# Spreading the split of tile 3's tokens over nine slices, and reading tile 0's partial results back a slice earlier

## The chip, the cores and the metric

The kernel runs on one core of one Trainium2 chip. The metric is the device time of one execution, in microseconds (us). The engines are named as in the profile: PE (TensorE matmul), PEld (its weight loads), DVE (VectorE), ACT (ScalarE), POOL (GpSimd) and SP (SyncE, which here only issues DMAs). Each engine works through its own list of instructions in order and waits on semaphores for the others.

## The reference

A windowed attention (32 keys wide; in the upper half of the heads every fourth key) feeds a feed-forward layer with a PReLU. Everything is float32.

```python
# q, k, v: (8 batches, 8 heads, 576 positions, 64)
scores = where(mask, q @ k.T / 8, -1e9)            # mask by head: plain window or dilated window
attn_out = (softmax(scores) @ v)                   # rows of x: 4608 tokens x 512
h = x @ w_in                                       # 512 x 2048
g = maximum(h, 0) + alpha * minimum(h, 0)
out = g @ w_out                                    # 2048 x 512
```

## The kernel before

**Precision.** PE multiplies in a reduced float format. So every operand is split in two parts of that format: a high part (a copy with a cast, on ACT) and a low part (the value minus its high part, on DVE). A product is three matmuls: high by high, high by low, low by high (`PASSES`).

**Tiles.** The 4608 tokens are nine tiles of 512. Tiles 0 to 2 are computed directly, slice by slice. A *slice* is one block of 128 of the 2048 hidden features for one tile: 12 matmuls of 128x512 for h (L495, `ffn_h`), the PReLU on ACT and DVE (L503 and L508, or L515 and L516), the split of g (L521 high on ACT, L526 low on DVE), and 12 matmuls for y (L543, `ffn_y`). There are 48 slices, numbered n = 0 to 47 in the list `slices`: six of tile 0, sixteen of tile 1, the last ten of tile 0 (n = 22 to 31), then tile 2 (n = 32 to 47). Tiles 3 to 8 follow in pairs, in the *paired stage*. It computes the products of two tiles at once with seven block products in place of eight (`Seven`, `PRODUCTS`, L728 and L1029), and so needs sums and differences of the two tiles' tokens, each split in high and low.

**What runs beside the slices.** Attention runs ahead of the tiles that use it. A pair of heads is *scored* in one slice: its scores on PE (L266), masked maxima on DVE (L318, L321, twice each, for two halves), exponentials on ACT (L331). One slice later come the division and the transpose on DVE (L338 to L346, tile `pt`). The pair is *valued* in the next slice that scores, or the one set for it: the values on PE (L361, tile `o`), copied out by ACT (L415, L422) and stored to DRAM as `kept`. Near the end of the list the scored slices are 37, 38, 40, 41, 43, 44, the valued ones 38, 40, 41, 43, 44, 46. Beside that, POOL sums weights for the paired stage, and ACT and DVE split those sums (L601, L606, L626, L630).

**What sets the order.** The order of every engine's instructions is the order in which the program is written; the pools only add waits for buffers. In the loop `for n in range(CUT, NS)`, round n issues h of slice n+1, the PReLU and the split of slice n+1 and the division of the pair scored in round n-1, then y of slice n-1, then the scores and values of round n with their maxima, exponentials and copies, the work of the weights, and at its very end `late_ops[n]`. With `NS = 48`, `NS - 9` is round 39. The PE banks "a0" to "a3" go round among h, the two score banks and the two value banks. So with one h, two score and two value banks in a round, the h of the next round takes the bank of that round's first scores and must wait until L318 has read them.

**The split of tile 3's tokens.** `token_parts(3)` returns 18 steps in three lists (`zeroth`, `first`, `second`): with k0, k1 the halves of tile 3 and z0, z1 those of tile 4 (each 128x1024), it splits k0 (named B11), k1 (B21), T1 = z0 - k0, T3 = z1 - z0, T2 = z1 - k0, B22 = z1 and T4 = k1 - T2. A difference is one DVE instruction (L707), a high part one on ACT (L710), a low part one on DVE (L713). `plan_parts` puts these 18 steps at the ends of rounds. Tile 3's tokens are loaded from DRAM in round 36, tile 4's in round 41 (L1093, `reload`).

**Tile 0's partial results.** The first six slices of tile 0 leave their sum of y in DRAM (`part`). When the last slice of tile 0 is multiplied (its y is issued in round 32), four DMAs read it back into `ob` (L541), and the function `end`, run in the same round, adds it to y on DVE (L551) and writes the result out (L556). Tile 2's first y, in round 33, uses the same four banks and waits for these four additions.

Of the kernel before, what the change touches and what calls it, by code (L numbers as in the profile page):

```python
# [31 lines left out]
NC = DM // P  # L32
# [34 lines left out]
def tile_window_attention_prelu_ffn(  # L67
# [12 lines left out]
    nc = tc.nc  # L80
# [18 lines left out]
    part = dram.tile([NC, P, TT], F32, name="part")  # L99
# [8 lines left out]
    def bank(side, shape, name):  # L108
        n = turn[side]
        turn[side] = n + 1  # L110
        return psp.tile(shape, F32, tag=f"{side}{n % 4}", name=name)
# [23 lines left out]
    def weight(which, a, f):  # L135
        k = next(k for k, (first, end) in enumerate(SPANS) if first <= f < end)
        i = 2 * which + a
        if (i, k) not in places:
            places[i, k] = place(i, k)
        return places[i, k][:, f - SPANS[k][0], :]  # L140
# [342 lines left out]
    def results(t):  # L483
        if t not in result:
            result[t] = const.tile([P, NC, TT], F32, tag=f"{XTAGS[t]}0", name=f"ob_{t}")
        return result[t]
# [3 lines left out]
    def ffn_h(t, f, first=0, end=NC):  # L490
        if first == 0:
            ms[t, f] = bank("a", [P, TT], f"h_{t}_{f}")
        for c in range(first, end):
            for n, (a, e) in enumerate(PASSES):
                nc.tensor.matmul(  # L495
                    ms[t, f], lhsT=weight(0, a, f)[:, c * P:(c + 1) * P], rhs=half(t, c)[:, e, :],
                    start=(c == 0 and n == 0), stop=(c == NC - 1 and n == 2))
# [30 lines left out]
    def ffn_y(t, f):  # L528
        first = (t, f) in ((0, 0), (0, CUT), (1, 0), (2, HALF))
        if first:  # L530
            ys[t] = [bank("y", [P, TT], f"y_{t}_{f}_{c}") for c in range(NC)]
        g = gs.pop((t, f))
        cut, rest = (t, f) == (0, CUT - 1), t == 0 and f == NF - 1
        last = cut or (t, f) in ((0, NF - 1), (1, NF - 1), (2, HALF - 1))
        if last:
            o = [
                att.tile([P, TT], F32, tag=("k", "q", "v", "pt")[c], name=f"ob_{t}_{f}_{c}") if cut else
                results(t)[:, c] for c in range(NC)]
        for c in range(NC):
            if rest:  # L540
                nc.sync.dma_start(out=o[c], in_=part[c])  # L541
            for n, (a, e) in enumerate(PASSES):
                nc.tensor.matmul(  # L543
                    ys[t][c], lhsT=weight(1, a, f)[:, c * P:(c + 1) * P], rhs=g[:, e, :],
                    start=(first and n == 0), stop=(last and n == 2),
                )

        def end():
            for c in range(NC):
                if rest:  # L550
                    nc.vector.tensor_tensor(out=o[c], in0=ys[t][c], in1=o[c], op=ALU.add)  # L551
                elif c % 2:
                    nc.vector.tensor_copy(out=o[c], in_=ys[t][c])
                else:
                    nc.scalar.copy(out=o[c], in_=ys[t][c])
                nc.sync.dma_start(  # L556
                    out=part[c] if cut else outT[c * P:(c + 1) * P, t * TT:(t + 1) * TT], in_=o[c])

        if last:
            ended.append(end)  # L560
# [140 lines left out]
    def token_parts(t):  # L701


        k0, k1, z0, z1 = raw(t, 0), raw(t, 1), raw(t + 1, 0), raw(t + 1, 1)

        def diff(out, x, y):
            return lambda: nc.vector.tensor_tensor(out=out, in0=x, in1=y, op=ALU.subtract)  # L707

        def high(name, x):
            return lambda: nc.scalar.copy(out=part_of(name, 0), in_=x)  # L710

        def low(name, x):
            return lambda: nc.vector.tensor_tensor(  # L713
                out=part_of(name, 1), in0=x, in1=part_of(name, 0).bitcast(F32), op=ALU.subtract)

        zeroth = [high("B11", k0), low("B11", k0), high("B21", k1), low("B21", k1)]
        first = [diff(k0, z0, k0), high("T1", k0), low("T1", k0)]
        second = [
            diff(z0, z1, z0), high("T3", z0), diff(k0, z1, k0), high("T2", k0), low("T3", z0),
            diff(k1, k1, k0), low("T2", k0), high("B22", z1), high("T4", k1), low("B22", z1), low("T4", k1),  # L720
        ]
        return zeroth, first, second
# [434 lines left out]
    late_ops = {}  # L1157

    def plan_parts():
        zeroth, first, second = token_parts(NSTD)  # L1160
        late_ops[NS - 9] = zeroth[:2]
        late_ops[NS - 5] = zeroth[2:] + first
        late_ops[NS - 3], late_ops[NS - 2], late_ops[NS - 1] = second[:5], second[5:8], second[8:]


    slices = [(0, f) for f in range(CUT)] + [(1, f) for f in range(NF)] + [(0, f) for f in range(CUT, NF)]
# [1 line left out]
    NS = len(slices)  # L1168
# [183 lines left out]
    for n in range(CUT, NS):  # L1352
        scored, valued, divided = (at.get(n) for at in (score_at, value_at, divide_at))
        whole = n + 1 == 2 * NF
        for op in put.pop(n, ()):
            op()
        if SCRATCH <= n < SCRATCH + NF:
            save(n - SCRATCH)
        if n + 1 < NS and not whole:
            ffn_h(*slices[n + 1])  # L1360
        if n <= SECOND - 2:

            ffn_sum(*slices[n])
            ffn_high(*slices[n])
            for w in late:
                w.low()
            words = [op for w in now for op in w.words()]
            for op in words[:1]:
                op()
            ffn_low(*slices[n])  # L1370
            if divided and n < SECOND - 2:
                divided.divisions()
                divided.turns()
            for op in words[1:]:
                op()
            if n + 1 <= SECOND - 2:
                ffn_relu(*slices[n + 1])
            late, now = now, [conversion() for _ in range(quota.pop(0) if quota else 0)]
            ahead()
            for w in late:  # L1380
                w.high()
        elif late:
            late.pop().low()
        if whole:
            ffn_y(*slices[n - 1])
            ffn_h(*slices[n + 1])
        if SECOND - 2 <= n < NS - 1:
            if n - 1 in score_at:
                ffn_parts(*slices[n + 1])
            else:  # L1390
                ffn_relu(*slices[n + 1])
                ffn_sum(*slices[n + 1])
            ffn_high(*slices[n + 1])
            if divided:
                divided.divisions()
                divided.turns()
            ffn_low(*slices[n + 1])
        if not whole:
            ffn_y(*slices[n - 1])
        if n in split_at:  # L1400
            combined_high(split_at[n])
        if n in cast_at:
            others_high(cast_at[n])
        if scored:
            scored.scores()
            pairs[pairs.index(scored) + 1].load_qk()
        if valued:
            valued.values()
            pairs[pairs.index(valued) + 1].load_v()
        if n in split_at:  # L1410
            put[n + 1].append(lambda i=split_at[n]: combined_store(i))
        if scored:
            scored.maxima()
            scored.exponentials(0, 5)
        while ended:
            ended.pop()()
        if valued:
            valued.highs()
            put[n + 1].append(valued.keep)
        if scored:  # L1420
            scored.exponentials(5)
        if valued:
            valued.lows(nc.scalar.copy)
        if n in split_at:
            combined_low(split_at[n])
        if n in cast_at:
            others_low(cast_at[n])
            put[n + 1].append(lambda i=cast_at[n]: others_store(i))
        if n == HALF + 1:
            pairs[2 * NC].load_qk()  # L1430
            pairs[2 * NC].load_v()
        if n in combine_at:
            combine(combine_at[n], "xB1" if n < 2 * NF - 1 else "xA1")
        if n in other_at:
            others(other_at[n], "xB0" if n <= 2 * NF - 1 else "xA0")
        for t, at in ((NSTD, NS - 12), (NSTD + 1, NS - 7)):
            for c in range(NC if n == at else 0):
                reload(t, c)
        if n == NS - 9:
            half(NSTD + 1, 0)  # L1440
            plan_parts()
        if n == NS - 2:
            nc.sync.dma_start(out=mask_sb, in_=masks[:, NMASK:2 * NMASK])
        for op in late_ops.pop(n, ()):
            op()
        if n >= NS - NRING + 2:
            feed()
# [76 lines left out]
```

## Time and profile before

| | |
|---|---|
| median of three runs | 855.82 us (853.35, 855.82, 857.77) |
| the profiled execution | 853.31 us, of which the span from first to last instruction is 850.8 us |
| PE busy | 826.2 us (97% of the span) |
| DVE busy | 650.6 us (76%) |
| ACT busy | 466.6 us (55%) |
| DMA | 194.90 MB, mean 229 GB/s |
| mean granted TensorE clock | 0.945 |

PE is busy nearly all the time, so the time is PE's work plus PE's pauses. A row of the view in order of time reads: start in us, duration in us, engine, line, operation, names written and read, shape, how many in a row (x12), and in brackets how long the engine sat idle before it and what released it. The durations of matmuls are modelled and overlap the next ones, so starts are the safer numbers on PE. The paired stage starts at 367 us.

### The profile page before, as it was taken

To read this page: it belongs to the slowest core of one execution; us is meant where nothing else is said; L and a number is where in the kernel's file an instruction comes from. 1 tells how busy PE (TensorE), PEld (TensorE's weight loads), DVE (VectorE), ACT (ScalarE), POOL (GpSimd) and SP (SyncE) were. 2 spreads that over 40 slices of the span, in tenths; PEclk is the share of its full clock that TensorE was granted. 3 is DMA by queue.
4 is the path that set the end of the run, shared out by engine and by line. 5 is a ranking of instruction groups with operands and counts; after the bars stand their busy time and mean duration, and the time that the engine had idled before them with its cause. 6 is when DMAs were issued, how large, how long until landed. Compare 5 with 4: busy or idle time off the path is not lost.

```text
span 850.8 us, 20392 instructions
## 1 busy us (share of the span) xinstructions
PE 826.2 (97%) x8014; PEld 671.7 (79%) x8014; DVE 650.6 (76%) x1087; ACT 466.6 (55%) x1276; POOL 86.5 (10%) x88
## 2 busy tenths in 40 slices
PE   8889999999999999799999999999999999999998
PEld 5668888878877887687888788878887888888886
DVE  5997866867667787679966998897379988944983
ACT  6895766645534466367635752674176436624640
POOL 0000000214683552000000000000000000000000
PEclk9999999999999999899999999999999999999999
DMA  7862479679766769286799598856876886667664
GB/s 243 281 203 86 164 236 310 216 237 294 214 215 236 263 217 338 94 296 195 230 313 314 154 314 299 272 170 214 242 215 190 290 287 198 195 190 196 193 193 157
DMA packets 131485, 194.90 MB, mean 229 GB/s; under 512 B 11582, under 2 KB 67518, under 8 KB 131390
## 3 DMA queue, kind: packets, MB, share of 16 engines
q1 hardware_dynamic: 131390, 193.60, 71.6%
q8 instruction: 63, 1.03, 0.5%
q14 instruction: 32, 0.26, 0.1%
HBM read 145.33 MB, written 48.23 MB: 228 GB/s over the span
## 4 chain that ended last, share of the span: by engine, by line
PE 78%; DVE 11%; ACT 5%; issue 2%; DMA 2%; SPq 1%; DVEq 0%; ACTq 0%
PE h L495 15%; PE qA L1029 14%; PE y L543 13%; PE pA L728 11%; PE qC L1029 7%; PE pC L728 5%; PE qB L1029 4%; PE o L361 3%; PE pB L728 3%; ACT pr L331 2%; PE s L266 2%; DVE held L787 1%; DMA ws<-w_in 1%; DVE pr L340 1%; DVE stage L780 1%
## 5 line engine op out<-in xcount | busy, mean ns | idle before, releaser
L495 PE MATMUL h<-x,w_dt.float32r 128*128 128x512 f32 x576 | 143.9, 399 | 2.6 <-DVE pr L318 1.0
L543 PE MATMUL y<-g,w_dt.float32r 128*128 128x512 f32 x576 | 138.6, 390 | 1.1 <-DVE ob L551 1.1
L495 PEld LDWEIGHTS h<-x,w_dt.float32r 128*128 128x128 f32 x576 | 107.8, 190 | 26.5 <-DVE pr L318 1.4
L543 PEld LDWEIGHTS y<-g,w_dt.float32r 128*128 128x128 f32 x576 | 107.8, 188 | 24.4 <-DVE ob L551 1.1
L331 ACT ACTIVATE pr<-pr,nm 128x64 f32<-128x64 f32 x216 | 72.4, 338 | 25.8 <-DVE nm L321 25.8
L773 ACT COPY stage<-pA 128x512 f32<-128x512 f32 x72 | 42.3, 587 | 47.6 <-PE pA L728 46.9
L728 PE MATMUL pA<-parts_w,ring_w 128*128 128x512 f32 x234 | 58.2, 392 | 0.3 <-ACT stage L773 0.3
L837 ACT CAST gp<-held 128x512 fp32r<-128x512 f32 x60 | 37.2, 620 | 35.7 <-DVE held L833 35.5
L728 PE MATMUL pA<-parts_w,ring_xA 128*128 128x512 f32 x222 | 55.4, 393 | 0.7 <-ACT stage L773 0.7
L728 PEld LDWEIGHTS pA<-parts_w,ring_w 128*128 128x128 f32 x234 | 43.6, 188 | 9.9 <-ACT stage L773 0.7
L503 ACT ACTIVATE m<-h 128x512 f32<-128x512 f32 x33 | 19.7, 598 | 57.5 <-PE h L495 49.0
L521 ACT CAST g<-m 128x512 fp32r<-128x512 f32 x48 | 29.7, 618 | 39.2 <-DVE m L516 20.7
L728 PEld LDWEIGHTS pA<-parts_w,ring_xA 128*128 128x128 f32 x222 | 41.2, 188 | 10.5 <-ACT stage L773 2.0
L526 DVE TENSOR_TENSOR g<-m,g 128x512 fp32r<-128x512 f32 x48 | 37.3, 778 | 15.5 <-ACT g L521 15.5
L780 DVE TENSOR_TENSOR stage<-pC,stage 128x512 f32<-128x512 f32 x48 | 33.0, 688 | 13.4 <-ACT stage L773 8.3
L954 ACT COPY py<-qA 128x512 f32<-128x512 f32 x24 | 13.8, 588 | 52.0 <-PE qA L1029 51.2
L1029 PE MATMUL qA<-gp,ring_xA 128*128 128x512 f32 x174 | 42.3, 390 | 0.0
L842 DVE TENSOR_TENSOR gp<-held,gp 128x512 fp32r<-128x512 f32 x60 | 40.7, 687 | 1.6 <-ACT gp L837 1.6
L331 ACT ACTIVATION_READ_ACCUMULATOR pr<-pr,nm 128x1 f32 x216 | 40.9, 189 | 0.0
L958 DVE TENSOR_TENSOR py<-qC,py 128x512 f32<-128x512 f32 x24 | 16.0, 688 | 31.0 <-PE qC L1029 24.7
L1029 PE MATMUL qA<-gp,ring_w 128*128 128x512 f32 x162 | 39.5, 389 | 0.0
L1029 PEld LDWEIGHTS qA<-gp,ring_xA 128*128 128x128 f32 x174 | 32.6, 188 | 7.0 <-DVE gp L842 0.2
(188 smaller groups left out, 1703.8 us busy)
## 6 DMA issues: line engine op xcount, KB each, us to landing
ring_w<-wS SPq DMA_DIRECT2D x69, 256.0 KB, 3.0
ring_xA<-wS SPq DMA_DIRECT2D x66, 256.0 KB, 3.0
ring_xA<-wY SPq DMA_DIRECT2D x40, 256.0 KB, 3.6
ring_w<-wY SPq DMA_DIRECT2D x36, 256.0 KB, 3.6
ring_g<-wS SPq DMA_DIRECT2D x33, 256.0 KB, 3.2
wO<-w_dt.float32r SPq DMA_DIRECT2D x32, 256.0 KB, 4.1
wS<-wc SPq DMA_DIRECT2D x16, 512.0 KB, 4.5
ring_w<-wO SPq DMA_DIRECT2D x31, 256.0 KB, 3.2
```

What stands on the lines that cost most here:

```text
L331: nc.scalar.activation(out=self.pr[:, r, :], in_=self.ps[r // CUT0][:, r % CUT0, :] if self.onto else self.pr[:, r, :], func=AF.Exp, bias= ...
L361: nc.tensor.matmul(self.po[u][e * D:(e + 1) * D, a:z, :], lhsT=self.v[rows, i, :], rhs=self.pt[rows, a * BK + (BQ if i else 0):z * BK - (B ...
L495: nc.tensor.matmul(ms[t, f], lhsT=weight(0, a, f)[:, c * P:(c + 1) * P], rhs=half(t, c)[:, e, :], start=(c == 0 and n == 0), stop=(c == NC ...
L521: nc.scalar.copy(out=g[:, 0, :], in_=ms[t, f])
L526: nc.vector.tensor_tensor(out=g[:, 1, :], in0=ms.pop((t, f)), in1=g[:, 0, :].bitcast(F32), op=ALU.subtract)
L543: nc.tensor.matmul(ys[t][c], lhsT=weight(1, a, f)[:, c * P:(c + 1) * P], rhs=g[:, e, :], start=(first and n == 0), stop=(last and n == 2),)
L728: nc.tensor.matmul(to, lhsT=w[:, (2 * a + c) * P:(2 * a + c + 1) * P], rhs=part_of(name, e)[:, c * TT:(c + 1) * TT], start=start and c == ...
L773: nc.scalar.copy(out=self.s(n), in_=self.A)
L780: nc.vector.tensor_tensor(out=self.s(n), in0=getattr(self, src), in1=self.s(to), op=ALU.add)
L837: nc.scalar.copy(out=self.pair(n)[:, 0], in_=self.whole(n))
L842: nc.vector.tensor_tensor(out=p[:, 1], in0=self.whole(n), in1=p[:, 0].bitcast(F32), op=ALU.subtract)
L1029: nc.tensor.matmul(to(q)[c], lhsT=w[:, k * P:(k + 1) * P], rhs=rhs[:, e], start=(i, q) in firsts and n == 0, stop=i == GP - 1 and n == 2, ...
```

## The change

Two things move; no instruction is added or removed. First, the four reads of `part` are taken out of `ffn_y` (round 32) and issued at the start of round 31. Second, the steps of `token_parts(3)`, which stood in lots of 2, 5, 5, 3 and 3 in rounds 39, 43, 45, 46 and 47, are dealt to all rounds from 39 to 47, mostly with the low part a round behind its high part.

```diff
@@ ffn_y @@
         for c in range(NC):
-            if rest:
-                nc.sync.dma_start(out=o[c], in_=part[c])
             for n, (a, e) in enumerate(PASSES):
@@ plan_parts @@
         zeroth, first, second = token_parts(NSTD)
-        late_ops[NS - 9] = zeroth[:2]
-        late_ops[NS - 5] = zeroth[2:] + first
-        late_ops[NS - 3], late_ops[NS - 2], late_ops[NS - 1] = second[:5], second[5:8], second[8:]
+        high_b11, low_b11, high_b21, low_b21 = zeroth
+        diff_t1, high_t1, low_t1 = first
+        diff_t3, high_t3, diff_t2, high_t2, low_t3, diff_t4, low_t2, high_b22, high_t4, low_b22, low_t4 = second
+        for back, ops in (
+                (9, (high_b11,)), (8, (low_b11,)), (7, (high_b21,)), (6, (low_b21, diff_t1)), (5, (high_t1,)),
+                (4, (low_t1, diff_t3)), (3, (high_t3, diff_t2)), (2, (low_t3, high_t2, diff_t4)),
+                (1, (low_t2, high_b22, high_t4, low_b22, low_t4))):
+            late_ops[NS - back] = ops
@@ the loop over n @@
         for op in put.pop(n, ()):
             op()
+        for c in range(NC if whole else 0):
+            nc.sync.dma_start(out=results(0)[:, c], in_=part[c])
```

**DVE, rounds 42 to 44, before.** `raw_xB0` holds tile 3's tokens, `raw_xB1` tile 4's, `parts` the split; `g_2_4` and `m_2_5` belong to tile 2's hidden blocks 4 and 5 (slices 44 and 45), `s_5_2` to the pair scored in round 43, `pr0` and `rs_5_2` to its softmax.

```order
L630 TENSOR_TENSOR ysum_3_4237<-ysum_3_4237 128x8x128
L508 SCALAR_TENSOR_TENSOR m_2_4_4462<-m_2_4_4462,bal_76,h_2_4_4449 128x512
L526 TENSOR_TENSOR g_2_4_4465<-m_2_4_4462,g_2_4_4465 128x512
L318 SCALAR_TENSOR_TENSOR pr0_78<-s_5_2_0_4483,mask_sb_74 128x320
L321 TENSOR_REDUCE nm_5_2_4567<-pr0_78 128x5
L318 SCALAR_TENSOR_TENSOR pr0_78<-s_5_2_1_4484,mask_sb_74 128x256
L321 TENSOR_REDUCE nm_5_2_4567<-pr0_78 128x4
L606 TENSOR_TENSOR wc3_1_4481<-wsum_xA1_3512,wc3_0_4480 128x1024
L713 TENSOR_TENSOR parts_w2_2_4587<-raw_xB0_3753,parts_w2_2_4587 128x1024
L707 TENSOR_TENSOR raw_xB0_3753<-raw_xB1_4096,raw_xB0_3753 128x1024
L713 TENSOR_TENSOR parts_w0_2_4591<-raw_xB0_3753,parts_w0_2_4591 128x1024
L515 TENSOR_SCALAR m_2_5_4612<-h_2_5_4599,al_75 128x512
```

Here the low part of B21, the difference T1 and the low part of T1 stand in a row at the end of round 43, ahead of L515.

The same place on DVE after the change (lines are shifted by two or more in the changed file):

```order
L628 TENSOR_TENSOR ysum_3_4235<-ysum_3_4235 128x8x128
L711 TENSOR_TENSOR parts_w2_2_4402<-raw_xB0_3753,parts_w2_2_4402 128x1024
L705 TENSOR_TENSOR raw_xB0_3753<-raw_xB1_4096,raw_xB0_3753 128x1024
L508 SCALAR_TENSOR_TENSOR m_2_4_4466<-m_2_4_4466,bal_76,h_2_4_4453 128x512
L526 TENSOR_TENSOR g_2_4_4469<-m_2_4_4466,g_2_4_4469 128x512
L318 SCALAR_TENSOR_TENSOR pr0_78<-s_5_2_0_4487,mask_sb_74 128x320
L321 TENSOR_REDUCE nm_5_2_4571<-pr0_78 128x5
L318 SCALAR_TENSOR_TENSOR pr0_78<-s_5_2_1_4488,mask_sb_74 128x256
L321 TENSOR_REDUCE nm_5_2_4571<-pr0_78 128x4
L604 TENSOR_TENSOR wc3_1_4485<-wsum_xA1_3512,wc3_0_4484 128x1024
L515 TENSOR_SCALAR m_2_5_4611<-h_2_5_4598,al_75 128x512
```

The low part of B21 and the difference T1 moved up to the end of round 42, ahead of L508; the low part of T1 moved down past L515, to the end of round 44.

**SP, rounds 31 and 32, before** (`k`, `q`, `v` are loads for coming pairs of heads, `wc` a split weight sum):

```order
L236 DMA k_4_0_3240<-kT 128x576
L237 DMA q_4_0_3241<-qT 128x576
L246 DMA v_3_3_3284<-vW 128x640
L225 DMA kept_3_86<-kept_3_3_2_3296 128x320
L225 DMA kept_4_87<-kept_4_3_2_3297 128x256
L541 DMA ob_0_3340<-part_81 128x512 x4
L556 DMA out<-ob_0_3340 128x512 x4
```

Before, the four reads stand directly ahead of the four writes of the result. On SP after the change:

```order
L1361 DMA ob_0_3171<-part_81 128x512 x4
L236 DMA k_4_0_3245<-kT 128x576
L237 DMA q_4_0_3246<-qT 128x576
L246 DMA v_3_3_3289<-vW 128x640
L225 DMA kept_3_86<-kept_3_3_2_3301 128x320
L225 DMA kept_4_87<-kept_4_3_2_3302 128x256
L554 DMA out<-ob_0_3171 128x512 x4
```

The reads moved ahead of five DMAs of round 31 and 32; the rest of the list is as it was.

## Rows read from the trace of the kernel before

**Rows 1.** PE in order of time, rounds 41 to 45 of the slices
```profile
310.95 3.02 PE L495 MATMUL h<-x,w_dt.float32r 128*128 128x512 f32 x12
...
316.62 1.21 PE L266 MATMUL s<-k,q 64*32 64x64 f32 x72
317.76 1.35 PE L361 MATMUL o<-pt,v 32*64 32x32 f32 x76
...
322.07 2.88 PE L543 MATMUL y<-g,w_dt.float32r 128*128 128x512 f32 x12
...
332.75 3.02 PE L495 MATMUL h<-x,w_dt.float32r 128*128 128x512 f32 x12
...
338.41 1.22 PE L266 MATMUL s<-k,q 64*32 64x64 f32 x72
345.05 2.35 PE L361 MATMUL o<-pt,v 32*64 32x32 f32 x76 [5.42 <-DVE pt L346]
347.32 4.96 PE L495 MATMUL h<-x,w_dt.float32r 128*128 128x512 f32 x12
352.12 2.90 PE L543 MATMUL y<-g,w_dt.float32r 128*128 128x512 f32 x12
```

**Rows 2.** Busy time by stretch: window, length, engines' busy time, PEclk, DMA share, GB/s
```profile
345.00:347.30 2.30, 2.25 (x76) 2.21 (x76) 2.21 (x5) 0.72 (x5) 0.00 (x0) 0.50 0.03 7
```

**Rows 3.** DVE in order of time, rounds 41 to 44
```profile
314.01 0.75 DVE L515 TENSOR_SCALAR m<-h,al 128x512 f32<-128x512 f32 x1 [2.01 <-PE h L495]
...
316.86 0.78 DVE L346 STREAM_TRANSPOSE pt<-pr 128x576 f32<-128x576 f32 x1
...
329.11 0.73 DVE L508 SCALAR_TENSOR_TENSOR m<-m,bal,h 128x512 f32<-128x512 f32 x1
...
331.15 0.49 DVE L318 SCALAR_TENSOR_TENSOR pr<-s,mask_sb 128x320 f32<-128x320 f32 x1
...
332.86 1.22 DVE L606 TENSOR_TENSOR wc<-wsum_xA,wc 128x1024 fp32r<-128x1024 f32 x1
336.97 1.23 DVE L713 TENSOR_TENSOR parts_w<-raw_xB,parts_w 128x1024 fp32r<-128x1024 f32 x1 [2.90 <-ACT parts_w L710]
338.12 1.22 DVE L707 TENSOR_TENSOR raw_xB<-raw_xB,raw_xB 128x1024 f32<-128x1024 f32 x1
340.45 1.23 DVE L713 TENSOR_TENSOR parts_w<-raw_xB,parts_w 128x1024 fp32r<-128x1024 f32 x1 [1.11 <-ACT parts_w L710]
...
344.21 0.78 DVE L346 STREAM_TRANSPOSE pt<-pr 128x576 f32<-128x576 f32 x1
```

**Rows 4.** PE in order of time, round 32: h behind a short wait
```profile
246.22 3.01 PE L495 MATMUL h<-x,w_dt.float32r 128*128 128x512 f32 x12 [0.83 <-DVE pr L318]
```

**Rows 5.** DMA of tile 4's tokens: issues by SP, then size and median us to landing
```profile
319.54 2.76 SPq L1093 DMA_DIRECT2D raw_xB<-kept  x4
raw_xB<-kept SPq DMA_DIRECT2D x4, 256.0 KB, 5.2
```

**Rows 6.** End of the slices: DVE's last result copies, first scores of the paired stage
```profile
366.78 1.36 DVE L553 COPY ob<-y 128x512 f32<-128x512 f32 x2
368.70 0.97 PE L290 MATMUL s<-lasting_k,lasting_q 64*32 64x64 f32 x72
```

**Rows 7.** Tile 2's first y on PE, and the scores behind it
```profile
255.32 1.63 PE L543 MATMUL y<-g,w_dt.float32r 128*128 128x512 f32 x6 [0.65 <-DVE ob L551]
...
259.05 1.21 PE L266 MATMUL s<-k,q 64*32 64x64 f32 x72
```

**Rows 8.** The additions on DVE, and the reads of part: issue by SP, landing
```profile
254.50 1.28 DVE L551 TENSOR_TENSOR ob<-y,ob 128x512 f32<-128x512 f32 x2
256.70 1.40 DVE L551 TENSOR_TENSOR ob<-y,ob 128x512 f32<-128x512 f32 x2 [0.93 <-DMA ob<-part]
251.30 1.88 SPq L541 DMA_DIRECT2D ob<-part  x4
ob<-part SPq DMA_DIRECT2D x4, 256.0 KB, 3.7
```

## The prediction

> **What bounds the kernel now.** I read the busy times first: PE is busy 826.2 us of 850.8, so only its pauses can be won. I then read the list of waits for PE's longest pause, and the view in order of time around it. The longest is in round 44: PE idles 5.42 us ahead of the values `o`, until DVE has transposed `pt` [rows 1]. The pause has a second price. The granted clock is 0.50 right behind it [rows 2], the lower of the two levels (1.2 GHz of 2.4), against a mean of 0.945, and while it is low the values take 2.35 us for 1.35 and the next h 4.96 us for 3.02 [rows 1].
>
> The whole loss is taken from starts, since the ends of matmuls are modelled. From the scores of round 44 to the y of round 45 PE needs 352.12 - 338.41 = 13.71 us. The same stretch of work two scored rounds earlier, with no such pause, needs 322.07 - 316.62 = 5.45 us [rows 1]. The difference, **8.26 us**, is the pause and the slow clock together.
>
> Who makes it? In round 43 three steps of the split stand on DVE between L606 and the PReLU of round 44. The low part of B21 waits 2.90 us for its high part, which ACT makes only behind the exponentials of that round; the difference T1 follows, and the low part of T1 waits another 1.11 us for ACT [rows 3]. Only behind them come the PReLU, the division and the transpose, which ends at 344.21 + 0.78 = 344.99. The values start 0.06 us later [rows 1, 3].
>
> A smaller pause lies in round 33. DVE idles 0.93 us for a read of `part` before the third of the four additions L551, which free the banks of tile 2's first y [rows 7, 8].
>
> **The change part by part.**
>
> *Round 43 is emptied.* Only the high part of T1 stays in it, on ACT. How does round 44 then run? Round 41 is the model: it has the same work (h, y, scores, values, division) and no late step on DVE before its transpose. There L515 starts 314.01 - 310.95 = 3.06 us behind the start of h, the transpose ends 316.86 + 0.78 - 314.01 = 3.63 us behind that, so 6.69 us behind h; the values start 6.81 us behind h, with no wait [rows 1, 3]. So if DVE is free when h of round 44 is done, the values do not wait, and all 8.26 us go. The margin is thin, 0.12 us. The row of the division's transpose before the change shows the same duration, so I keep the model.
>
> *Round 42 is loaded.* The low part of B21 and the difference T1 now stand ahead of L508, L526 and L318 of round 43. Two such steps cost 2 x (338.12 - 336.97) = 2.30 us of DVE [rows 3]; their inputs are there (the high part is made in round 41 on ACT; tile 4's tokens are issued at 319.54 and land some 5.2 us later, by about 328 for the last [rows 5], and T1 is reached at about 330.3). DVE has no gap there, since L508 is queued right behind the weight split L630. Who waits? The h of round 44 needs the bank of round 43's first scores, so it waits for the first L318. That ends at 331.15 + 0.49 = 331.64, and h starts at 332.75 [rows 1, 3]: a slack of 1.11 us. So PE is delayed by 2.30 - 1.11 = **1.19 us**. (The values of round 43 also wait for L508, which frees their bank; that wait lies inside the same delay.) The bounds are 0, if the values and the scores leave more slack than these rows show, and 2.30, if none of it is slack. I take 1.19, which is worked out from the neighbouring rows.
>
> Does the rest of the lag run on into round 44? DVE finishes L606 at 332.86 + 1.22 = 334.08 before, so at 336.38 with the lag. The delayed h starts at 332.75 + 1.19 = 333.94 and L515 follows it by 3.06 us, at 337.00. So 0.62 us of DVE are left and the lag ends there. With this cover gone, each us of lag would be a us of wait for the values.
>
> *Rounds 39 to 41.* The low part of B11 leaves round 39 and goes to the end of round 40, where DVE idles 2.01 us until h is done [rows 3]; 1.2 us fit in. The high part of B21 comes to the end of round 41 on ACT, ahead of a cast whose low part DVE takes only behind the transpose. Cost nothing. If that cover were gone, 1.2 us.
>
> *Rounds 44 to 47.* Round 44 gets two DVE steps, 2.30 us, behind the last maxima. DVE waits there for h before the change too, and what follows, the division for round 46, is wanted three blocks of 12 matmuls later. Cost nothing. At the very end one DVE step more than before (1.15 us) stands between the last low part of g and the two copies of tile 2's results. These end at 366.78 + 1.36 = 368.14, and the scores that take over their banks start at 368.70 [rows 6], a slack of 0.56 us. But DVE reaches this place earlier than before, since the differences T3 and T2 no longer hold up the last PReLU. I take nothing; without that cover 0.6 us.
>
> *The earlier reads.* SP issues them in round 31. Before, their issue starts at 251.30 and the last addition waits until 256.70, 3.7 us being the median from issue to landing [rows 8]. The tile they fill is free when h of slice 31 is done, which is issued in round 30; the h at 246.22 is already that of round 32 [rows 4]. They pass five DMAs on SP: a k, a q and a v load and two stores of `kept`, which move back by the 1.88 us of issue, with their users a round away. So the third addition starts straight behind the second, 0.92 us earlier (at 254.50 + 1.28 = 255.78 instead of 256.70 [rows 8]). On PE, y starts at 255.32 and takes 2.88 us where nothing holds it [rows 1], so the scores could start at 258.20 in place of 259.05: 0.85 us [rows 7]. The wait of 0.65 us ahead of that y stays, because DVE is busy until 254.50. I take **0.9 us**; bounds 0 and 0.93.
>
> **The clock, and a rule that speaks against the change.** After the change PE has short waits in place of the long one, about 0.4 to 1.2 us in rounds 43 and 44. A wait of 0.83 us stands ahead of the h at 246.22, and that h takes 3.01 us, full speed [rows 4]. So by the rows, short waits leave the clock alone.
>
> The Trainium skill ("TensorE: Matmul & The Clock Gate", section "A second HAM failure mode: psum-queue depth-cycling") says that frequent micro-idling between groups of matmuls makes the gate swing between its two levels, with lost throughput. The row above does not show it for a single wait; by that rule the slow stretch would come back at round 44.
>
> What the slow stretch costs is in the rows: the values to h take 347.32 - 345.05 = 2.27 us, against some 1.3 us, and h to y 4.80 against 2.85, 2.9 us together [rows 1].
>
> **The sum.** 8.26 - 1.19 + 0.9 = 8.0 us. The slices are followed by PE-bound work that starts when they end, so a gain there should reach the end. Against the profiled execution: 853.31 - 8.0 = 845.3 us. That execution is at the low end of the runs (853.35 to 857.77); the median, 855.82, is 2.5 us higher, and less 8.0 gives 847.8. I take the middle, **846.5 us**.
>
> **The rivals.**
> - *The clock falls all the same.* The short waits of rounds 43 and 44 trigger the low level once: 2.9 us come back. 846.5 + 2.9 = 849.4. For it: the two waits lie close together. Against it: rows 4.
> - *The lag runs on.* The 0.62 us left in round 43 and the margin of 0.12 us are not enough, and DVE's 2.30 us meet the values of round 44 again: 846.5 + 2.3 = 848.8. For it: both margins come from single rows. Against it: DVE waits for PE in every round of the model.
> - *The gain is lost behind the slices.* The paired stage is paced by its weight loads and not by the end of the slices, so what is saved before 367 us is waited for later; or the long pause has another cause than the late steps. Then some 2 us remain at most: about 853.5. Against it: its first steps have their data before they start, and the list of PE's waits names no DMA there.
> - *Slower.* T1 now wants tile 4's tokens in round 42 instead of 43. If they land after 330.3, DVE stands with L508, L526 and L318 behind it, and PE with h of round 44; each us late is a us lost, and a pause as long as the old one brings the slow clock again. The loads land some 2 us before. They would have to come about 5 us after 330.3 to eat the gain with the clock's 2.9 us; 3 us more, a wait of 8 us, gives 846.5 + 8 + 2.9 = 857.4. Against it: 5.2 us to landing, with nothing in the rows near 11.
>
> **How the numbers follow.** Forecast 0.70, clock 0.08, lag 0.08, lost behind 0.10, slower 0.04. A measurement of this kernel can tell about 0.5%, 4.3 us, from no change. The first three cases lie below 851.5: faster 0.86, same 0.10, slower 0.04. Range: with the new cost at 0 and the whole 0.93 us the profiled execution would be at 853.31 - 9.2 = 844.1; with the new cost at 2.30, 0.6 at the end and nothing from the reads 853.31 - 5.4 = 847.9, or 850.4 against the median. With a little room for the spread of the runs: 843.5 to 850.5.
>
> **What would show it.** In the changed profile: no wait of `o` for `pt` over 0.3 us in round 44; h and values at 3.0 and 1.35 us there; a new wait of h in round 44 for L318, and of the values in round 43 for L508, together 1 to 1.5 us; DVE's L551 without a wait for a DMA; the paired stage starting near 359 us. A pause over 2 us in rounds 42 to 45, or a clock of 0.5 there, would make it wrong; so would a PE that waits in the paired stage by what it gained.

## The result

The changed kernel takes 845.23 us (median of four runs, 843.94 to 847.35) against 855.30 us for the kernel before (median of four runs, 853.35 to 857.77). The ratio is 0.9883, with a 95% interval from 0.9848 to 0.9918: faster by 1.2%. The forecast was 846.5 us in a range of 843.5 to 850.5.

The profiled execution of the changed kernel is the slowest of its four, 847.35 us with a span of 845.6 us. PE is busy 825.9 us, about as before (826.2). This sum hides two things that cancel: matmuls at the low clock count as longer busy time, in round 44 before, and near 30 and 52 us in this execution of the changed kernel (below).

PE in order of time in the changed kernel, rounds 32 and 33 and then 43 to 45, with the first matmul of the paired stage (start, duration, engine, line, what, how many; in brackets the idle time before it and its releaser). The y line is L541 here, L543 before.

```profile
248.94 3.02 PE L495 MATMUL h<-x,w_dt.float32r 128*128 128x512 f32 x12 [0.43 <-DVE pr L318]
...
258.06 3.00 PE L541 MATMUL y<-g,w_dt.float32r 128*128 128x512 f32 x12 [0.67 <-DVE ob L549]
260.99 1.21 PE L266 MATMUL s<-k,q 64*32 64x64 f32 x72
...
334.23 1.35 PE L361 MATMUL o<-pt,v 32*64 32x32 f32 x76 [0.62 <-DVE m L508]
336.01 3.02 PE L495 MATMUL h<-x,w_dt.float32r 128*128 128x512 f32 x12 [0.42 <-DVE pr L318]
...
341.68 1.21 PE L266 MATMUL s<-k,q 64*32 64x64 f32 x72
342.81 1.35 PE L361 MATMUL o<-pt,v 32*64 32x32 f32 x76
344.10 3.02 PE L495 MATMUL h<-x,w_dt.float32r 128*128 128x512 f32 x12
346.96 2.88 PE L541 MATMUL y<-g,w_dt.float32r 128*128 128x512 f32 x12
...
362.06 1.52 PE L726 MATMUL pA<-parts_w,ring_w 128*128 128x512 f32 x6
```

Set beside [rows 1], the values at 342.81 have no bracket: the 5.42 us are gone, and values and h take 1.35 and 3.02 us again, full speed. In their place stand the waits at 334.23 and 336.01. Set beside [rows 7], tile 2's first y is one run of 12 matmuls; only the wait ahead of it is left.

DVE in order of time in the changed kernel, the same place as [rows 3]:

```profile
331.17 1.21 DVE L711 TENSOR_TENSOR parts_w<-raw_xB,parts_w 128x1024 fp32r<-128x1024 f32 x1
332.31 1.21 DVE L705 TENSOR_TENSOR raw_xB<-raw_xB,raw_xB 128x1024 f32<-128x1024 f32 x1
333.44 0.74 DVE L508 SCALAR_TENSOR_TENSOR m<-m,bal,h 128x512 f32<-128x512 f32 x1
...
335.47 0.48 DVE L318 SCALAR_TENSOR_TENSOR pr<-s,mask_sb 128x320 f32<-128x320 f32 x1
...
339.06 0.75 DVE L515 TENSOR_SCALAR m<-h,al 128x512 f32<-128x512 f32 x1 [0.67 <-PE h L495]
...
341.70 0.78 DVE L346 STREAM_TRANSPOSE pt<-pr 128x576 f32<-128x576 f32 x1
```

The two steps of round 42 run without a wait, and L508 follows them. L515 waits for PE again, 0.67 us, where before DVE was late.

For the experiments one measure is used throughout: the **stretch**, the time from the start of h of slice 32 (issued in round 31) to the first matmul of the paired stage. It is 367.25 - 239.64 = 127.61 us before and 362.06 - 242.76 = 119.30 us after the change: 8.31 us less. The paired stage, from there to the end of the span, is 483.55 us before and 483.54 us after. So the stretch holds the whole gain that the change can claim by the traces. The paired stage is the same and the programs do not differ ahead of the stretch, so the rest of the 10 us between the medians is put down to the start of the program (below).

### The profile page after: what moved, and what is told of

Read it like the earlier page. It is cut to its first block, busy times and chain, and to the rows that moved or that the text cites. A ratio compares the mean times of both kernels' runs of the same rounds, so it can differ in the third digit from the quotient of the medians.

```text
span 845.6 us, 20392 instructions
## 1 busy us (share of the span) xinstructions
PE 825.9 (98%) x8014; PEld 671.3 (79%) x8014; DVE 652.3 (77%) x1087; ACT 466.3 (55%) x1276; POOL 87.0 (10%) x88
## 4 chain that ended last, share of the span: by engine, by line
PE 81%; DVE 10%; ACT 4%; issue 2%; DMA 1%; SPq 0%; DVEq 0%; ACTq 0%
PE h L495 15%; PE qA L1027 15%; PE y L541 14%; PE pA L726 11%; PE qC L1027 7%; PE pC L726 6%; PE qB L1027 4%; PE o L361 3%; PE pB L726 3%; PE s L266 2%; DVE held L785 1%; ACT pr L331 1%; DVE stage L778 1%; DVE gp L840 1%; DVE py L956 1%
## 5 line engine op out<-in xcount | busy, mean ns | idle before, releaser
L541 PE MATMUL y<-g,w_dt.float32r 128*128 128x512 f32 x576 | 138.3, 389 | 0.7 <-DVE ob L549 0.7
L541 PEld LDWEIGHTS y<-g,w_dt.float32r 128*128 128x128 f32 x576 | 108.0, 188 | 23.5 <-issue 1.1
L526 DVE TENSOR_TENSOR g<-m,g 128x512 fp32r<-128x512 f32 x48 | 37.9, 789 | 15.5 <-ACT g L521 15.5
```

Of the source, the lines that this page charges most:

```text
L526: nc.vector.tensor_tensor(out=g[:, 1, :], in0=ms.pop((t, f)), in1=g[:, 0, :].bitcast(F32), op=ALU.subtract)
L541: nc.tensor.matmul(ys[t][c], lhsT=weight(1, a, f)[:, c * P:(c + 1) * P], rhs=g[:, e, :], start=(first and n == 0), stop=(last and n == 2),)
```

## The experiments

### The spread without the earlier reads

```diff
-        for c in range(NC if whole else 0):
-            nc.sync.dma_start(out=results(0)[:, c], in_=part[c])
...
         for c in range(NC):
+            if rest:
+                nc.sync.dma_start(out=o[c], in_=part[c])
```

> The steps of the split spread as in the change, the four reads of part left in round 32. Measure: the stretch from h of round 31 (slice 32) to the first matmul of the paired stage, 127.61 us before the change and 119.30 after it. My theory (the spread takes the pause of round 44 away and gives about 1.2 us back in rounds 43 and 44; the reads are worth 0.8 us by themselves): 120.1 us, a DVE wait of about 0.9 us for the read of part, no wait of o for pt over 0.3 us in round 44, and a time about 7.2 us under before. Rival (the reads carry a good part of the gain): over 121.5 us. Rival (most of the 10 us between the medians comes from the start of the program and not from this stretch): the stretch as said, and a time that differs from the changed kernel's by more than 2 us.

846.96 us; ratio to before 0.9926 (0.9898 to 0.9955). The stretch is 362.33 - 242.07 = 120.26 us, so the spread alone is worth 127.61 - 120.26 = 7.35 us. Its median lies 6.12 us under the 853.08 us of the 17 runs of the kernel before that were timed beside it; 7.2 was expected. The DVE rows of this kernel show the wait for the read again, and its PE rows show what it costs:

```profile
256.93 1.27 DVE L551 TENSOR_TENSOR ob<-y,ob 128x512 f32<-128x512 f32 x2
258.81 1.36 DVE L551 TENSOR_TENSOR ob<-y,ob 128x512 f32<-128x512 f32 x2 [0.60 <-DMA ob<-part]
```

```profile
257.76 1.63 PE L543 MATMUL y<-g,w_dt.float32r 128*128 128x512 f32 x6 [0.67 <-DVE ob L551]
259.55 1.68 PE L543 MATMUL y<-g,w_dt.float32r 128*128 128x512 f32 x6 [0.16 <-DVE ob L551]
261.16 1.21 PE L266 MATMUL s<-k,q 64*32 64x64 f32 x72
```

The values of round 44 do not wait. The two rivals fall: the stretch is 120.26 - 119.30 = 0.96 us longer than the changed kernel's, and the medians differ by less than 2 us.

Not all of the 0.96 us belongs to the additions. From tile 2's first y to the scores PE takes 261.16 - 257.76 = 3.40 us here and 260.99 - 258.06 = 2.93 in the changed kernel, which is 0.47 us. Another 0.38 us lies earlier, ahead of h of slice 33, which waits 0.81 us here and 0.43 there. That wait goes with the length of one DVE instruction, the L526 just ahead of the L318 that h waits for. DVE before and after the change:

```profile
244.67 1.10 DVE L526 TENSOR_TENSOR g<-m,g 128x512 fp32r<-128x512 f32 x1 [0.68 <-ACT g L521]
```

```profile
247.79 0.69 DVE L526 TENSOR_TENSOR g<-m,g 128x512 fp32r<-128x512 f32 x1 [0.69 <-ACT g L521]
```

In all ten traces the wait is this duration less 0.26 to 0.27 us: 1.10 and 0.83 before, 1.08 and 0.81 here, 1.13 and 0.86 in the kernel with four added steps, which has the early reads. L526 is long where one of POOL's weight sums is still running when it starts: it then ends 0.55 us behind that sum, at 245.77 behind 245.22 before. After the change the sum ends at 247.81, as L526 starts. So this wait hangs on how POOL and DVE meet, and no run here shows that the reads set this.

### The earlier reads without the spread

The edit of the change to the reads, on the kernel before.

> The four reads of part in round 31 as in the change, the split as before. My theory: the third of the four additions no longer waits for a DMA, the scores of round 33 follow the start of tile 2's first y by 2.9 us instead of 3.73, the pause of about 5.4 us in round 44 and the slow clock behind it stay, and the stretch from h of slice 32 to the paired stage is 126.8 us (127.61 before). The time is then about 0.8 us under before, which three rounds can hardly tell. Rival (the earlier reads also shorten the later pause): a stretch under 125 us.

852.29 us; ratio 0.9993 (0.9976 to 1.001), which is no difference that timing can tell. The additions no longer wait, and the pause stays. PE in order of time in this kernel:

```profile
254.72 2.99 PE L541 MATMUL y<-g,w_dt.float32r 128*128 128x512 f32 x12 [0.67 <-DVE ob L549]
257.64 1.21 PE L266 MATMUL s<-k,q 64*32 64x64 f32 x72
...
343.14 2.35 PE L361 MATMUL o<-pt,v 32*64 32x32 f32 x76 [5.33 <-DVE pt L346]
345.41 4.01 PE L495 MATMUL h<-x,w_dt.float32r 128*128 128x512 f32 x12
349.26 2.89 PE L541 MATMUL y<-g,w_dt.float32r 128*128 128x512 f32 x12
```

The stretch, 125.00 us, missed the expectation of 126.8 and lies at the edge of what the rival wanted. The pause itself is as long as before, 5.33 us. What is shorter is the work at the low clock: h to y takes 349.26 - 345.41 = 3.85 us here, 4.80 in [rows 1], which is 0.95 us of the 2.61. The clock fell at another place of the pause. Granted clock in a late part of the pause, here and then in the kernel before (window, length, engines, PEclk, DMA share, GB/s):

```profile
340.80:343.10 2.30, 0.00 (x0) 0.00 (x0) 2.20 (x6) 0.62 (x1) 0.00 (x0) 0.50 0.11 42
```

```profile
342.70:344.60 1.90, 0.00 (x0) 0.00 (x0) 1.80 (x5) 0.62 (x1) 0.00 (x0) 0.95 0.07 25
```

0.95 is the full level in that trace. Here part of the low stretch is spent while PE stands still. One trace does not tell whether the earlier reads or chance set this. Up to the scores of round 33 this kernel is 1.15 us ahead of before, of which 0.36 stand at h of slice 33 already; another 0.47 us is a wait for `pt` in round 38 that does not occur here. The pair above, where all else is the changed kernel, is the better measure of the reads: 0.47 us at the additions.

### The kernel before, a second trace

No edit.

> The kernel before, once more, for a second trace. My theory (the stretch from h of slice 32 to the paired stage and the paired stage itself are the same in each execution, and the spread of the runs, 853.35 to 857.77, comes from the start of the program, where the changed kernel's profiled execution lost 2.7 us against that of before at a low granted clock near 30 and 52 us): the stretch is 127.6 us within 0.5, the paired stage 483.5 us within 0.5, and the start of h of slice 32 lies anywhere between 239 and 244 us. Rival (the pause of round 44 varies from run to run, so that the gain does too): the stretch differs by over 1 us.

One run of 852.79 us. The stretch is 367.31 - 239.84 = 127.47 us, the paired stage 851.0 - 367.31 = 483.69, the pause 5.12 us. The stretch and the paired stage lie within 0.2 us of the first trace and the pause within 0.3, so the pause does not vary much between these two executions. The wait for the read does: 0.52 us here, 0.93 in [rows 8]. DVE and then PE at the additions:

```profile
256.61 1.36 DVE L551 TENSOR_TENSOR ob<-y,ob 128x512 f32<-128x512 f32 x2 [0.52 <-DMA ob<-part]
```

```profile
255.64 3.38 PE L543 MATMUL y<-g,w_dt.float32r 128*128 128x512 f32 x12 [0.66 <-DVE ob L551]
258.94 1.21 PE L266 MATMUL s<-k,q 64*32 64x64 f32 x72
```

From y to the scores it is 3.30 us here and 3.73 in the first trace. This trace alone says nothing on the spread of the starts; the traces together do. In the ten traces of this study h of slice 32 starts anywhere from 239.38 to 244.35 us, though the compute engines run the same instructions in the same order in all of them ahead of round 31.

### One step in each round

```diff
-                (9, (high_b11,)), (8, (low_b11,)), (7, (high_b21,)), (6, (low_b21, diff_t1)), (5, (high_t1,)),
+                (9, (high_b11,)), (8, (low_b11,)), (7, (high_b21,)), (6, (diff_t1,)), (5, (low_b21, high_t1)),
```

> The changed kernel, but the low part of B21 stands at the end of round 43 instead of round 42, so that DVE has one step of 1.15 us ahead of the PReLU of round 43 and not two. My theory (the h of round 44 waits for L318, which two steps push back by 2.30 us against a slack of 1.11; one step fits into it): the waits of o for L508 (0.62 us) and of h for L318 (0.42 us) in rounds 43 and 44 fall to under 0.2 us together, the values of round 44 still don't wait over 0.3 us for pt, and the stretch from h of slice 32 to the paired stage is 118.2 us (119.30 in the changed kernel). The time is about 1.1 us under the changed kernel. Rival (round 43 has no room for a step, the lag only moves to the transpose of round 44): o waits about 1 us for pt in round 44 and the stretch stays at 119 to 119.5 us.

844.78 us (842.38 to 848.62); ratio to before 0.9907 (0.9876 to 0.9938). The stretch is 359.79 - 241.81 = 117.98 us, 1.32 less than the changed kernel's. PE in order of time:

```profile
332.25 1.35 PE L361 MATMUL o<-pt,v 32*64 32x32 f32 x76
333.61 3.02 PE L495 MATMUL h<-x,w_dt.float32r 128*128 128x512 f32 x12
...
339.27 1.21 PE L266 MATMUL s<-k,q 64*32 64x64 f32 x72
340.50 1.35 PE L361 MATMUL o<-pt,v 32*64 32x32 f32 x76
```

The waits of 0.62 and 0.42 us in rounds 43 and 44 are gone, and the values of round 44 follow their scores by 1.23 us, as good as without a wait. So it was the two steps in round 42 that cost the changed kernel its 1.2 to 1.3 us, through L508 and L318, and round 43 has room for one step. The run times of this kernel and the changed one overlap, and the medians differ by 0.45 us where 1.1 was expected; only the stretch tells them apart, by one trace of each.

### The high parts early, two DVE steps back in round 43

```diff
-                (9, (high_b11,)), (8, (low_b11,)), (7, (high_b21,)), (6, (low_b21, diff_t1)), (5, (high_t1,)),
+                (9, (high_b11,)), (8, (low_b11,)), (7, (high_b21,)), (5, (low_b21, diff_t1, high_t1)),
```

> The changed kernel, but the low part of B21 and the difference T1 stand at the end of round 43 again, as before the change; the high part of B21 stays in round 41 on ACT and the low part of T1 in round 44. So two of the three DVE steps of the old lot are back in their place, and only the waits for ACT (2.90 and 1.11 us before) and one step are gone. My theory (the pause came mostly from DVE standing in its queue for high parts that ACT made behind its exponentials): the two steps cost 2.30 us of DVE against about 1.8 us of slack, o waits 0.4 to 0.6 us for pt in round 44, the waits in rounds 43 and 44 for L508 and L318 go, the clock stays up, and the stretch from h of slice 32 to the paired stage is 118.6 us (119.30 in the changed kernel, 117.98 with one step in each round). Rival (the work of the steps on DVE made the pause, their waits did not): a pause of some 4 us in round 44, the slow clock behind it, and a stretch of 124 us or more.

One run of 847.26 us, with a late start (h of slice 32 at 243.48); the stretch is 361.68 - 243.48 = 118.20 us. The first two of the three DVE steps of [rows 3] stand where they stood, and there is hardly a pause. DVE and then PE in order of time:

```profile
335.59 1.22 DVE L604 TENSOR_TENSOR wc<-wsum_xA,wc 128x1024 fp32r<-128x1024 f32 x1
336.73 1.22 DVE L711 TENSOR_TENSOR parts_w<-raw_xB,parts_w 128x1024 fp32r<-128x1024 f32 x1
337.86 1.22 DVE L705 TENSOR_TENSOR raw_xB<-raw_xB,raw_xB 128x1024 f32<-128x1024 f32 x1
339.00 0.74 DVE L515 TENSOR_SCALAR m<-h,al 128x512 f32<-128x512 f32 x1
```

```profile
341.14 1.21 PE L266 MATMUL s<-k,q 64*32 64x64 f32 x72
342.45 1.35 PE L361 MATMUL o<-pt,v 32*64 32x32 f32 x76
```

The first step starts when L604 ends; in [rows 3] it waited 2.90 us. The values follow the scores by 1.31 us against 1.14 without any wait. The rival, that the work of the steps made the pause, wanted 4 us there. So the 4.01 us that DVE waited for ACT's high parts, and not the steps that it carried, were the main part of the 5.42 us; the third step, which this kernel has in round 44, is 1.15 us. The expectation of 0.4 to 0.6 us for the wait was too high by some 0.3.

### Two and four steps more in round 43

The second kernel has 4 in place of 2.

```diff
-                (5, (high_t1,)),
+                (5, (high_t1,) + 2 * (low_b21,)),
```

> The changed kernel with two more DVE steps at the end of round 43 (the low part of B21 computed again, twice, 2.30 us). My theory (0.67 us of DVE are free there and the rest is a wait of o for pt): a wait of 1.3 to 1.7 us in round 44, the values and h behind it at full clock (1.35 and 3.0 us), a stretch of 120.7 us (119.30 without). Rival (a pause of this size is enough to bring the clock down): values at 2.3 us, and 2 to 3 us more.

> The changed kernel with four more DVE steps at the end of round 43 (4.6 us). My theory on the wait: 3.6 to 3.9 us of o for pt in round 44. On the clock the runs so far leave it open: waits up to 2.1 us left it up and one of 5.4 us brought it down for 4 to 6 us. If it stays up, the stretch is 123.0 us; if it falls, the values take 2.3 us and the stretch is 125 to 126 us.

The stretches are 364.75 - 244.35 = 120.40 us and 364.43 - 239.75 = 124.68 us (119.30 without the added steps); the run times, 850.33 and 850.14 us, hide this behind starts 4.6 us apart. PE in order of time around the values of round 44, first with two steps more, then with four:

```profile
345.47 1.35 PE L361 MATMUL o<-pt,v 32*64 32x32 f32 x76 [1.27 <-DVE pt L346]
346.75 3.06 PE L495 MATMUL h<-x,w_dt.float32r 128*128 128x512 f32 x12
349.65 2.88 PE L541 MATMUL y<-g,w_dt.float32r 128*128 128x512 f32 x12
```

```profile
343.66 2.03 PE L361 MATMUL o<-pt,v 32*64 32x32 f32 x76 [3.80 <-DVE pt L346]
345.61 3.88 PE L495 MATMUL h<-x,w_dt.float32r 128*128 128x512 f32 x12
349.32 2.88 PE L541 MATMUL y<-g,w_dt.float32r 128*128 128x512 f32 x12
```

A wait of 1.27 us leaves values and h at 1.35 and 3.06 us; one of 3.80 us brings them to 2.03 and 3.88. The granted clock in the second kernel, by stretch (window, length, engines, PEclk, DMA share, GB/s):

```profile
343.66:345.60 1.94, 1.94 (x76) 1.89 (x76) 1.87 (x5) 0.41 (x3) 0.00 (x0) 0.61 0.03 8
345.60:347.60 2.00, 2.00 (x7) 1.60 (x6) 2.00 (x3) 2.00 (x14) 0.00 (x0) 0.53 0.41 102
347.60:349.40 1.80, 1.80 (x10) 1.47 (x9) 0.55 (x1) 1.38 (x9) 0.00 (x0) 1.00 0.56 214
```

So late DVE work comes through to PE nearly one for one beyond the free 0.67 us, and the price jumps where the pause brings the clock to its low level: from two to four added steps the wait grows by 2.53 us and the stretch by 4.28 us. Two of the expectations were missed by a little: the wait with two steps was to be 1.3 us at least, and the stretch with four, the clock low, 125 us at least.

### The additions ahead of the division

The kernel with one step in each round, and in round 32 the y of slice 31 and `end` are called ahead of the division, so that DVE makes the four additions first.

```diff
             ffn_high(*slices[n + 1])
+            if n == 2 * NF:
+                ffn_y(*slices[n - 1])
+                ended.pop()()
             if divided:
                 divided.divisions()
...
-        if not whole:
+        if not whole and n != 2 * NF:
             ffn_y(*slices[n - 1])
```

> The kernel with one step in each round (stretch 117.98 us, 844.78 us), and in round 32 the four additions on DVE are put ahead of the division and the low part of g. My theory (with the reads early, the 0.67 us that tile 2's first y still waits is DVE's own order): that wait goes, and of the 0.67 us at least a part comes through; DVE has little free in round 33, so h of slice 35 may wait for L318 by 0.2 to 0.4 us. Stretch 117.3 to 117.8 us. Rival (DVE is the bound there): the scores of round 33 start earlier by 0.67 us but h of slice 35 stands where it stood, stretch 118.0 us.

845.86 us (844.68 to 846.38); ratio to before 0.9909 (0.9887 to 0.9931). The stretch is 360.53 - 242.61 = 117.92 us, as good as unchanged. PE and DVE in order of time:

```profile
257.20 2.88 PE L541 MATMUL y<-g,w_dt.float32r 128*128 128x512 f32 x12
260.01 1.21 PE L266 MATMUL s<-k,q 64*32 64x64 f32 x72
...
263.52 3.01 PE L495 MATMUL h<-x,w_dt.float32r 128*128 128x512 f32 x12 [1.01 <-DVE pr L318]
```

```profile
261.49 1.57 DVE L526 TENSOR_TENSOR g<-m,g 128x512 fp32r<-128x512 f32 x1 [0.68 <-ACT g L521]
```

The 0.67 us ahead of y are gone, and 1.01 us stand ahead of the next h instead. The stretch is the one that the rival named, but its reason, that DVE is the bound there, is not shown. This L526 takes 1.57 us, against 0.69 in the kernel with one step in each round; that is 0.88 of the 1.01 us. POOL's weight sums run beside it, from 259.87 to 262.51, and it ends 0.55 us behind them, at 263.06. In the other kernel POOL starts them at 262.94, behind that L526. What the order of the additions is worth without this overlap stays open.

## Why the prediction was right

**The pause and the slow clock, 8.26 us.** Right, with the mechanism named: the scores of round 44 to the y of round 45 take 346.96 - 341.68 = 5.28 us after the change, 13.71 before, so 8.43 us went. The cause, DVE standing in line for high parts from ACT, is shown by the kernel that gives back two of the three steps but not the waits (stretch 118.20 us).

**The new cost in rounds 42 to 44, 1.19 us.** Right in size and place. Both foreseen waits are there (0.62 and 0.42 us). From the scores of round 43 to h of round 44 PE takes 336.01 - 332.40 = 3.61 us, 332.75 - 330.32 = 2.43 before, so 1.18 us more; taking one step out of round 42 brings 1.32 us.

**No lag into round 44.** Right: 0.62 us of free DVE were worked out, 0.67 are shown by the L515 row. The margin behind the transpose was not 0.12 but 0.33 us (it ends at 341.70 + 0.78 = 342.48, the values start at 342.81). The two added steps confirm both from the other side: 2.30 us of work less 0.67 and 0.33 is 1.30, and 1.27 us came through.

**The earlier reads, 0.9 us.** Right in sum only, and by luck: 0.96 us of stretch by the pair of kernels that differ in the reads alone. At the additions themselves the prediction counted 0.85 us, from a single trace in which DVE waited 0.93 us for the read. With late reads y to scores takes 3.73, 3.30 and 3.40 us in three traces, with early ones 2.93 in the changed kernel, so the additions give 0.37 to 0.80 us, and 0.47 by the pair. The other part comes from h of slice 33, which waits 0.43 us and not 0.83 in the changed kernel. This was not foreseen, and it goes with the length of the L526 ahead of it, as the experiment without the reads showed. In the other kernels with early reads this wait is anything between 0.42 and 0.86 us, so it isn't a fixed gain of the reads.

**Nothing at the end of the slices, nothing lost behind them.** Right: the paired stage is 483.5 to 483.7 us in every trace, whatever the stretch ahead of it.

**The clock rival** fell for the waits that the change makes, and the four-step kernel shows where it would have held: at 3.80 us of pause. The Trainium skill's rule on short idling ("TensorE: Matmul & The Clock Gate", section "A second HAM failure mode: psum-queue depth-cycling") did not bite in rounds 43 and 44: two waits of 0.62 and 0.42 us there, and h at 3.02 us.

**The absolute time.** The sum was 8.0 us, the stretch gained 8.31, and the medians differ by 10.07 us. The 1.8 us between the last two are not seen in the stretch or behind it. They are within the spread of the starts, 5 us over the traces. In larger samples the kernel before has medians of 853.08 us (17 runs) and 853.37 us (11 runs), some 2 us under the four runs beside which the changed kernel was timed. The choice of 2.5 us between the profiled execution and the median of three runs was thus a choice on that spread, and the result, 845.23, came out at the lower end of it; that the middle of the two came so close is luck. Against the larger samples the other kernels gain 1.2 to 2.2 us less by their medians than by their stretches: 6.12 for 7.35 us (spread alone), 0.79 for 2.61 (reads alone), 8.30 for 9.63 (one step in each round), 7.51 for 9.69 (additions first). The stretches are of one trace each; whether the draw of the starts explains all of this stays open. The sign that the paired stage would start near 359 us was off for the same reason: it starts at 362.06 because this execution came to h of slice 32 at 242.76 us and not at 239.64.

Where much of those 3 us was lost the clock column shows. The start of the changed kernel's profiled execution, by stretch (window, length, PE, PEld, DVE, ACT and POOL busy, PEclk, DMA share, GB/s):

```profile
20.00:30.00 10.00, 7.83 (x237) 5.21 (x235) 9.69 (x25) 8.79 (x40) 0.00 (x0) 1.00 0.85 311
30.00:36.00 6.00, 6.00 (x34) 4.55 (x37) 5.45 (x14) 5.28 (x25) 0.00 (x0) 0.72 0.75 235
...
50.00:56.00 6.00, 6.00 (x56) 4.83 (x48) 5.83 (x14) 4.57 (x23) 0.00 (x0) 0.72 0.74 280
```

The clock is at its low level for part of two windows, 0.72 on average. In the kernel before the same two windows show 0.95, which is the full level in that trace, and in its second trace 1.00. The instructions ahead of round 31 are the same in all. The clock is not the whole of it: the kernel with the additions first came to h of slice 32 at 242.61 us with 1.00 in both windows; there PE idled 2.09 us near 30 us, for nothing that the profile shows.

No version measured here is faster than the changed kernel by more than the runs can tell: one step in each round has 1.3 us less stretch, and 844.78 us against 845.23.

## What to carry to other kernels

A low part belongs a round behind its high part when the high part is made at the end of another engine's long list: of the old pause of 5.42 us, 4.0 were DVE waiting in its queue for ACT, and with these waits and one step gone the other two steps cost 0.2 us. Before a step is moved up, look for what stands behind it in the queue: the step's price is its length less the slack of the first waiter there, here 2.30 less 1.11 us, and with one step in that round and one in the next nothing was lost. And measure a small change by the stretch that it touches, from a start that all versions share; here the start of the program varied by 5 us, more than half of the gain.

## What the runs showed of the hardware

- In the slices a wait of 1.27 us left the following h at 3.06 us, and the stretch grew by 1.10 us, no more than the wait. Behind pauses of 3.80, 5.12, 5.33 and 5.42 us the granted clock was 0.50 to 0.61 (1.2 GHz of 2.4 for all or most of the stretch), and they cost more than their length. Nothing between 1.27 and 3.80 us was tried there.
- How much work falls into the low clock is not set by the length of the pause alone: values and h behind a pause of 5.33 us took 6.12 us from start to start, behind 5.12 and 5.42 us 7.04 and 7.07 us, against 4.15 at full speed. In the first case the clock was at 0.50 already while PE stood still.
- In the start of the program, where PE was busy 7.83 of 10 us and waited at most 1.4 us at a time, the clock also fell. It fell in some executions and not in others: in the kernel with four added steps PE was busy 7.50 us in the same window, idled 1.44 us once, and the clock stayed at 1.00. So rows of a single short wait were too little to rule it out in general. There the rule of the Trainium skill named above agrees with the trace of the changed kernel.
- The granted clock of a busy stretch reads 0.95 in one trace of the kernel before and 1.00 in the other traces, and the 12 matmuls of an h take 3.02 us in both.
- L526, a DVE instruction that reads two 128x512 tiles and writes one, took 0.69 us where no sum of POOL was running at its start or where one was about to end. Where one had longer to run, L526 took up to 1.57 us and ended 0.55 us behind POOL's sum: 245.77 behind 245.22 before, 263.06 behind 262.51 with the additions first, and likewise in the other traces. No run moved POOL's work on purpose.
